# Two planner constants: chunk 0's tail admitted 34 steps before the end of attention, at 1,200 planned ns a block

## The chip, the core and the metric

The kernel runs as one program on one core of a Trainium2 chip. The engines are TensorE (PE, with its weight loads listed apart as PEld), VectorE (DVE), ScalarE (ACT), GpSimd (POOL) and SyncE (SP, which here only issues DMAs). The metric is the device time of one execution in microseconds; all times below are microseconds unless marked ns.

## The reference

For `x` of 2048 rows by 512 columns, six rows of modulation come from a condition vector: `sa, ca, ga, sb, cb, gb = silu(c) @ w_mod`. Then there are two halves.

```python
h = layernorm(x) * (1 + ca) + sa
x = x + ga * attention(h)          # 32 heads of width 16, then @ wo
h = layernorm(x) * (1 + cb) + sb
x = x + gb * mixer(h)

# mixer(h):
g  = gelu(layernorm(h) @ w1)
h1 = h + shift(g) @ w2             # the four column quarters moved by +1, -1, +2, -2 rows
return h1 + gelu(layernorm(h1) @ w3) @ w4
```

## The kernel before, in words

**Chunks, units, steps, blocks.** The 2048 rows are four chunks of 512 queries. Attention handles one chunk and one pair of heads at a time: a unit, 64 in all, chunk 3's last. A unit is 16 steps, one for each 128 keys, and a step has two halves, one for each head. The main loop takes three halves at a time; I call that a block. A block issues on PE the score matmuls of its halves (`sc`, L1012), the matmuls that find the row maxima 24 steps ahead (`mb`, L996), and then matmuls of probabilities and values (`pv`, L1086 for the high parts, L1083 for the low parts) of steps that lie two blocks back. ACT takes the exponential of each `sc` (L1008), DVE the maximum of each `mb` (L992), and each step needs one more pass that cuts out the low part of the probabilities, `p_low`: on POOL (L1061) or on ACT (L156), wherever the planner's clock is ahead. L1083 reads what that pass writes. In the last 24 steps there is no `mb` any more.

**The tail.** What comes after attention is done chunk by chunk by the generator `tail(ci)`. Chunk 0's begins inside attention. It transposes chunk 0's attention output (`xT<-ident,osb`, L1247; ACT L353 and DVE L349 split each result in two parts), multiplies by `wo` (48 matmuls `wo`, lines 359, 361 and 363 in turn, twelve for each of four row tiles that I number 0 to 3), and runs a chain for each row tile on DVE, POOL and ACT: add (L1406), statistics (L370, L371, L1353), POOL's power `trs` (L1356), centring (L1415), scaling (L1418), statistics again, POOL L1356, L1360 and L1361, and ACT's `xn` (L1367). Two row tiles together are then transposed (`xT<-ident,xn`) and multiplied by `w1` (matmuls named `w`, twelve for each bank of results). Each bank goes through the gelu chain: ACT square L1456, DVE L1457, ACT tanh L1458, DVE L1438, ACT copy L1459, POOL L1460. The three buffers for `xn` make row tile 3 wait in the plan until row tiles 0 and 1 have been transposed.

**Order.** All engines' programs are written out by a planner, `Sched`, which keeps a clock for each engine and puts operations in the order in which it thinks they will be ready. On the chip each engine runs its program in that order and waits on semaphores. Between blocks the planner may put in pieces of the generators, on credit: every block adds to `due`, and when `due` reaches a threshold, `fill(due)` lets the generators issue about so many ns of TensorE work.

```python
late = s0 >= NS - T0S
due += RATE3 if late else RATE if s0 < NS // NC else RATE2
if due >= (BURST3 if late else BURST if s0 < NS // NC else BURST2):
    sch.fill(due)
    due = 0.0
...
if blk and blk[0] <= 2 * (NS - T0S) <= blk[-1]:
    sch.add(tail(0))
```

`NS` is 1024 steps, `BURST3` is 1300, so that with 1,000 or 1,200 a block every second block has a fill. A generator that is not ready (a buffer taken, a flag not set, no PSUM bank) gives nothing, whatever the credit. Banks are shared: seven rotate among `sc`, `mb` and what the generators use.

**Names of blocks.** I count blocks back from the last one with scores, block 0 (it has two `sc`). Before the change the first fill with tail work stands at the end of block -20, and block -16 is the last with `mb`.

Of the kernel before, what the change touches and what calls it, by code (L numbers as in the profile page):

```python
# [82 lines left out]
X1T = 5  # L83
XBF = 4
XBT = 4
T0S = 30
T0L = 140
T0W = 3000.0
RATE3 = 1000.0
BURST3 = 1300.0  # L90
BF, BR = 2, 3
HOME = "rfrr"
# [238 lines left out]
def kernel(ctx, tc, A_x, A_wqkv, A_wo, B_w1, B_w2, B_w3, B_w4, c, w_mod, out):  # L331
# [942 lines left out]
    def tail_loads():  # L1274
        rings["0"] = Ring(FRONT, [], "r")
        for _ in range(BR):
            rings["0"].add([("wr", BR)])
            yield sch.wait(T0W)
        for t in range(TPC):
            x1t[t] = fa.tile([P, D], F32, name="x1", tag="x1", bufs=X1F)  # L1280
            act.dma_start(x1t[t], x_d[t * P:(t + 1) * P])
# [320 lines left out]
    for k, blk in enumerate(blocks + [[]] * (LAG + CPER)):  # L1602
# [52 lines left out]
        elif sch.gens:  # L1655
# [3 lines that stand above are left out]
# [14 lines left out]
        if blk and blk[0] <= 2 * (NS - T0L) <= blk[-1]:  # L1673
            sch.add(tail_loads())
        if blk and blk[0] <= 2 * (NS - T0S) <= blk[-1]:
            sch.add(tail(0))
# [54 lines left out]
```

## Time and profile before

| | us |
|---|---|
| median of three runs | 2020.98 |
| lowest and highest run | 2018.84 and 2023.25 |
| the profiled execution, its own time | 2021.44 |
| its span, first to last instruction | 2019.7 |
| PE busy | 1934.4 (96%) |
| DVE busy | 1656.3 (82%) |
| POOL busy | 1571.9 (78%) |
| ACT busy | 1510.2 (75%) |

The span has three parts: the projections up to about 100, attention to about 1533, and the tails of the four chunks. A row of the timeline gives the start, the duration, the engine, the line and operation, the tiles, the shapes and the count, and in brackets how long the engine stood idle before it and what released it. A row of a view by windows gives the stretch, its length, each engine's busy time with its number of instructions, the granted clock of TensorE as a share of full speed, the share of the DMA engines and GB/s.

### The profile page before, as it was taken

The numbers are of one execution on the slowest core, as the hardware profiler recorded it, in microseconds if no ns is written. First come the engines' busy times: TensorE is split into PE (matmuls) and PEld (weight loads), VectorE is DVE, ScalarE is ACT, GpSimd is POOL, SyncE is SP. The second block draws the span as 40 slices with busy tenths as digits, with TensorE's granted clock in tenths as the row PEclk, the third lists the DMA queues.
The fourth block names the chain that finished last, engine by engine and source line by source line (L and its number), as shares of the span: only waits on it lengthen the run. The fifth ranks groups of instructions, "written<-read, shape, count | busy, mean of one in ns | idle before, by whom it ended". The sixth has DMA issues, their size and how long they took to land.

```text
span 2019.7 us, 41655 instructions
## 1 busy us (share of the span) xinstructions
PE 1934.4 (96%) x14456; PEld 1162.1 (58%) x14456; DVE 1656.3 (82%) x2979; ACT 1510.2 (75%) x3085; POOL 1571.9 (78%) x1488
## 2 busy tenths in 40 slices
PE   7999999999999999999999999999998999999999
PEld 5755545454444444444444444444455878898998
DVE  6398888879999999999999999999975886556443
ACT  6438987768999999999999999999985544344443
POOL 6349988879999999999999999999996554435222
PEclk9989999999999999999999999999999999999999
DMA  8777675445343434444443435354414676553541
GB/s 295 233 204 192 151 187 155 135 130 124 86 92 87 91 88 83 96 82 97 81 98 75 104 72 107 72 136 126 99 46 158 230 261 265 226 200 116 201 153 68
DMA packets 185508, 278.01 MB, mean 138 GB/s; under 512 B 117104, under 2 KB 127856, under 8 KB 169008
## 3 DMA queue, kind: packets, MB, share of 16 engines
q1 hardware_dynamic: 181792, 267.20, 49.1%
q10 hardware_dynamic: 2304, 4.20, 0.6%
q0 software_dynamic: 1200, 3.93, 0.5%
q8 instruction: 115, 1.88, 0.4%
q14 instruction: 97, 0.79, 0.1%
HBM read 211.81 MB, written 62.91 MB: 136 GB/s over the span
## 4 chain that ended last, share of the span: by engine, by line
PE 61%; DVE 16%; ACT 9%; issue 6%; POOL 4%; DMA 3%; SPq 0%; ACTq 0%; POOLq 0%; DVEq 0%
PE mb L996 13%; DVE mx L992 12%; PE pv L1086 9%; PE sc L1012 8%; ACT pt L1008 7%; PE w L363 5%; PE w L359 5%; PE w L361 5%; PE pv L1083 4%; PE ot L1113 3%; POOL pt L1061 2%; PE xT L1247 1%; POOL trs L1356 1%; PE v L359 1%; DMA wr<-Ws 1%
## 5 line engine op out<-in xcount | busy, mean ns | idle before, releaser
L1061 POOL TENSOR_SCALAR pt<-pt 128x1024 f16<-128x1024 uint16 x953 | 1248.3, 1367 | 79.9 <-ACT pt L1008 76.7
L992 DVE TENSOR_REDUCE mx<-mb 128x1 f32<-128x512 f32 x2048 | 1250.0, 681 | 72.7 <-PE mb L996 63.5
L1008 ACT ACTIVATE pt<-sc 128x512 int32<-128x512 f32 x2048 | 1060.9, 614 | 123.5 <-PE mb L996 97.1
L996 PE MATMUL mb<-kst,qtl 62*128 62x512 f32 x2048 | 781.1, 461 | 20.5 <-ACT pt L1008 10.0
L1012 PE MATMUL sc<-qtl,kst 64*128 64x512 f32 x2048 | 739.3, 449 | 4.6 <-DVE mx L992 1.8
L996 PEld LDWEIGHTS mb<-kst,qtl 62*128 62x128 f32 x2048 | 358.9, 193 | 233.7 <-ACT pt L1008 160.4
L1012 PEld LDWEIGHTS sc<-qtl,kst 64*128 64x128 f32 x2048 | 336.6, 185 | 185.4 <-DVE mx L992 118.7
L1086 PE MATMUL pv<-pt,vst 128*32 128x512 f16 x4096 | 384.8, 397 | 20.6 <-ACT ac L1103 20.6
L1460 POOL TENSOR_TENSOR g<-sq,g 128x256 fp32r<-128x256 f32 (+1 forms) x124 | 96.8, 785 | 188.9 <-ACT g L1459 176.6
L1083 PE MATMUL pv<-pt,vst 128*32 128x512 f16 (+1 forms) x2048 | 220.8, 389 | 2.5 <-POOL pt L1061 2.4
L1086 PEld LDWEIGHTS <-vst 128*32 128x32 bf16 x4096 | 91.8, 93 | 227.2 <-issue 208.8
L361 PE MATMUL w<-A,wr 128*128 128x256 f32 (+1 forms) x520 | 153.4, 295 | 0.3 <-DVE A L349 0.3
L359 PE MATMUL w<-A,wr 128*128 128x256 f32 (+1 forms) x520 | 153.2, 295 | 0.3 <-ACT A L353 0.3
L363 PE MATMUL w<-A,wr 128*128 128x256 f32 (+1 forms) x520 | 153.1, 294 | 0.0
L1456 ACT ACTIVATE sq<-w 128x256 f32<-128x256 f32 (+1 forms) x130 | 52.1, 401 | 127.0 <-PE w L363 117.5
L363 PE MATMUL w<-wr,g 128*128 128x512 f32 x270 | 106.5, 394 | 3.1 <-POOL g L1460 3.1
L359 PE MATMUL w<-wr,g 128*128 128x512 f32 x270 | 106.9, 396 | 1.8 <-DMA wr<-Ws 1.8
L361 PE MATMUL w<-wr,g 128*128 128x512 f32 x270 | 106.1, 393 | 0.0
L1438 DVE SCALAR_TENSOR_TENSOR sq<-sq,w 128x256 f32<-128x256 f32 (+1 forms) x130 | 58.1, 449 | 56.5 <-ACT sq L1458 56.3
L359 PEld LDWEIGHTS w<-A,wr 128*128 128x128 f32 x520 | 98.7, 190 | 1.7 <-ACT A L353 0.5
L361 PEld LDWEIGHTS w<-A,wr 128*128 128x128 f32 x520 | 98.7, 190 | 1.6 <-DVE A L349 0.5
L363 PEld LDWEIGHTS w<-A,wr 128*128 128x128 f32 x520 | 98.6, 190 | 0.5 <-issue 0.5
(156 smaller groups left out, 2131.6 us busy)
## 6 DMA issues: line engine op xcount, KB each, us to landing
wr<-Ws SPq DMA_DIRECT2D x66, 1024.0 KB, 5.2
vst<-Vs SPq DMA_DIRECT2D x64, 768.0 KB, 5.7
kst<-Ks SPq DMA_DIRECT2D x126, 384.0 KB, 6.1
Ws<-wr SPq DMA_DIRECT2D x14, 1024.0 KB, 5.0
qtl<-Qs SPq DMA_DIRECT2D x128, 96.0 KB, 4.3
Vs<-vt SPq DMA_DIRECT2D x32, 384.0 KB, 4.2
Ks<-qk SPq DMA_DIRECT2D x16, 512.0 KB, 3.8
Qs<-qk SPq DMA_DIRECT2D x16, 512.0 KB, 3.0
```

The source lines that it names most:

```text
L359: te.matmul(o, lh, rh, start=first, stop=False)
L361: te.matmul(o, lh, rl, start=False, stop=False)
L363: te.matmul(o, ll, rh, start=False, stop=last)
L992: end = sch.crit("D", 605, e + PX, lambda: dve.reduce_max(mxs[u][:, j, g, c:c + 1], b, axis=AX.X))
L996: return ready, lambda: te.matmul(b, lhs, kst[u % 3][r, c * CH:(c + 1) * CH], start=True, stop=True), after
L1008: ea = sch.crit("A", 480, e + PX, lambda: act.activation(pt[s][:, j], b, AF.Exp))
L1012: return ready, lambda: te.matmul(b, kst[u % 3][r, kt * P:(kt + 1) * P], qst[u][r], start=True, stop=True), after
L1061: e_low[s] = XP["G"] + sch.crit("G", 1345, ready, lambda: pool.tensor_scalar(o, i, 0.5, 1.0, op0=OP.mult, op1=OP.mult))
L1083: te.matmul(acc[r:r + n, :], v[:, kt + i, c:c + n].bitcast(F16), pt[s + i].bitcast(F16)[:, j, 0::2], start=False, stop=kt == NKT - 2, skip ...
L1086: te.matmul(acc[r:r + 32, :], v[:, kt, r:r + 32], pt[s].bitcast(F16)[:, j, 1::2], start=kt == 0, stop=False, skip_group_check=True)
L1113: te.matmul(b[:, t * n:(t + 1) * n], ac[:, t * P:(t + 1) * P], smat.rearrange("p j d -> p (j d)"), start=True, stop=True)
L1460: ("G", cG(n), lambda: pool.tensor_tensor(lo, sq, hi, op=OP.subtract)), (None, 0, end), bank=b)
```

## The change

```diff
-T0S = 30
+T0S = 34
...
-RATE3 = 1000.0
+RATE3 = 1200.0
```

`T0S` sets both when `tail(0)` is admitted and when the credit rate becomes `RATE3`. The instructions are the same except for one `p_low`, which is on ACT (L156) now and was on POOL (L1061). Their order differs only from block -21 to a few microseconds after block 0; before and behind that, every engine's program is the same but for numbers in names of buffers.

PE, the end of block -17 and the start of block -16 (`osb` is chunk 0's attention output), first before and then now:

```order
L1083 MATMUL pv<-pt,vst 32x512
L1247 MATMUL xT<-ident,osb_105 128x128 x7
L1012 MATMUL sc<-qtl_1103,kst_1105 128x512
L996 MATMUL mb<-kst_147,qtl_145 128x512 x2
L1012 MATMUL sc<-qtl_1103,kst_1105 128x512 x2
```

```order
L359 MATMUL wo<-wr,A 128x512
L361 MATMUL wo<-wr,A 128x512
L363 MATMUL wo<-wr,A 128x512
L1012 MATMUL sc<-qtl_1103,kst_1105 128x512
L996 MATMUL mb<-kst_147,qtl_145 128x512 x2
L1012 MATMUL sc<-qtl_1103,kst_1105 128x512 x2
```

The rows of `wo` are the last three of nine, which with a unit's `ot` (L1113) before them now stand ahead of block -16; the `ot` stood one block earlier. The sixteen transposes of `osb` stood 5, 3, 1 and 7 behind blocks -20, -19, -18 and -17, and stand 8, 5 and 3 behind blocks -21, -20 and -19 now. The 48 `wo` stood 9, 9, 9, 9, 9 and 3 behind blocks -15, -13, -11, -9, -3 and -1, and stand 9, 11, 11, 5, 11 and 1 behind blocks -17, -15, -13, -11, -3 and -1 now. The eight transposes of `xn` of row tiles 0 and 1 stood behind block -5 and stand four each behind blocks -7 and -6 now. From the fifth `w` that stood behind the last `pv` on, PE's program is the same again: twelve `w` stood between the last `pv` and the following `ot`, and eight do now.

ACT in blocks -7 to 0 (`ot`, `sm` are a unit's closing sums), before and now:

```order
L1120 ACTIVATE sm<-ot 128x136
L1008 ACTIVATE pt<-sc 128x512 x6
L353 ACTIVATE A<-xT 128x2x256 x2
L1008 ACTIVATE pt<-sc 128x512 x6
L1367 ACTIVATE xn<-xb,trs 128x512
L1008 ACTIVATE pt<-sc 128x512 x8
```

```order
L1120 ACTIVATE sm<-ot 128x136
L353 ACTIVATE A<-xT 128x2x256
L1008 ACTIVATE pt<-sc 128x512 x3
L156 ACTIVATE pt<-pt 128x1024
L1367 ACTIVATE xn<-xb,trs 128x512
L353 ACTIVATE A<-xT 128x2x256
L1008 ACTIVATE pt<-sc 128x512 x15
```

The `p_low` of a step of block -7 stands on ACT now, among the exponentials of the next block, and POOL has one fewer.

DVE at the end of attention, from the add of row tile 3 (`x_21950`) on; `w_24626`, `w_24671` (`w_24672` before) and `w_24685` are the first, second and third bank of `w1` results. Before and now:

```order
L1406 TENSOR_TENSOR x_21950<-x_21950,wo 128x512
L370 BN_STATS tst<-x_21950 128x6
L371 BN_AGGR tmv<-tst 128x2
L1353 TENSOR_SCALAR tmv<-tmv 128x1
L1415 SCALAR_TENSOR_TENSOR xb<-x_21950,tmv,cbrow 128x512
L1457 SCALAR_TENSOR_TENSOR sq<-sq,w_24626 128x256
L1457 SCALAR_TENSOR_TENSOR sq<-sq,w_24672 128x256
L1418 SCALAR_TENSOR_TENSOR xb<-xb,trs,sbrow 128x512
L1438 SCALAR_TENSOR_TENSOR sq<-sq,w_24626 128x256
L1438 SCALAR_TENSOR_TENSOR sq<-sq,w_24672 128x256
L370 BN_STATS tst<-xb 128x6
```

```order
L1406 TENSOR_TENSOR x_21950<-x_21950,wo 128x512
L1457 SCALAR_TENSOR_TENSOR sq<-sq,w_24626 128x256
L1438 SCALAR_TENSOR_TENSOR sq<-sq,w_24626 128x256
L1457 SCALAR_TENSOR_TENSOR sq<-sq,w_24671 128x256
L370 BN_STATS tst<-x_21950 128x6
L371 BN_AGGR tmv<-tst 128x2
L1353 TENSOR_SCALAR tmv<-tmv 128x1
L1415 SCALAR_TENSOR_TENSOR xb<-x_21950,tmv,cbrow 128x512
L1438 SCALAR_TENSOR_TENSOR sq<-sq,w_24671 128x256
L1418 SCALAR_TENSOR_TENSOR xb<-xb,trs,sbrow 128x512
L1457 SCALAR_TENSOR_TENSOR sq<-sq,w_24685 128x256
```

Row tile 3's first statistics stood directly behind its add and stand behind three gelu operations of the first two banks now; its second statistics follow the third bank's L1438 now. ACT's `xn` of row tile 3 stands behind the fourth bank's L1459 now, and stood ahead of its L1458.

## The prediction

> **What bounds the kernel now.** I read the engines' busy time by windows first, then POOL's `p_low`, then the timeline of PE, DVE and ACT around the end of attention. First comes a stretch inside attention, second the last 40 us up to POOL's last `p_low`; the third row counts `p_low` alone in that stretch (POOL busy, clock, DMA), the fourth is the page's group of all of them.
>
> ```profile
> 1440.00:1460.00 20.00, 19.53 (x171) 9.19 (x170) 19.39 (x35) 18.25 (x38) 19.63 (x18) 1.00 0.38 81
> 1493.30:1533.30 40.00, 37.82 (x276) 19.75 (x276) 18.42 (x36) 26.82 (x54) 39.30 (x41) 1.00 0.25 79
> ```
>
> ```profile
> 1493.30:1533.30 40.00, 33.34 (x24) 1.00 0.25 79
> ```
>
> ```profile
> L1061 POOL TENSOR_SCALAR pt<-pt 128x1024 f16<-128x1024 uint16 x953 | 1248.3, 1367 | 79.9 <-ACT pt L1008 76.7
> ```
>
> While maxima are still taken, PE (19.5 of 20), DVE (19.4) and POOL (19.6) are all near full. In the last 40 us of attention DVE falls to 18.4 of 40, ACT to 26.8, PE stays at 37.8, and POOL is full: 39.3, of it 33.3 in 24 `p_low`, 1.39 each. So in this stretch POOL's queue sets the end of attention, and PE's fills run beside it. What the change can move is decided there and in the few microseconds behind.
>
> More planned credit does not mean more tail work ahead of the end: the program of PE is the same again four matmuls behind the last `pv`, so nothing substantial leaves the time after attention. The change reorders, and each reordering has a price.
>
> **Part 1: fills before block -16 make POOL wait.** The timeline of PE and POOL around block -16 before, and one pair of ACT rows for the lag from scores to exponentials:
>
> ```profile
> 1485.18 1.08 PE L1113 MATMUL ot<-smat,ac 128*128 128x34 f32 x8
> 1488.11 0.98 PE L1247 MATMUL xT<-ident,osb 128*128 128x128 f32 x7
> 1489.02 0.49 PE L1012 MATMUL sc<-qtl,kst 64*128 64x512 f32 x1
> 1491.87 0.50 PE L359 MATMUL wo<-wr,A 128*128 128x512 f32 x1
> 1494.14 0.73 PE L1012 MATMUL sc<-qtl,kst 64*128 64x512 f32 x3
> ```
>
> ```profile
> 1488.36 0.40 POOL L1124 TENSOR_TENSOR osb<-sm,rc 128x128 f32<-128x128 f32 x1 [1.75 <-DVE rc L1128]
> 1488.73 3.92 POOL L1061 TENSOR_SCALAR pt<-pt 128x1024 f16<-128x1024 uint16 x3
> 1493.12 0.20 POOL L1045 TENSOR_TENSOR nm<-mf,nm 128x8 fp32r<-128x8 f32 x1 [0.47 <-ACT nm L1044]
> 1493.30 6.60 POOL L1061 TENSOR_SCALAR pt<-pt 128x1024 f16<-128x1024 uint16 x5
> 1530.99 0.95 POOL L1356 TENSOR_TENSOR trs<-tmv,mhalf 128x1 f32<-128x1 f32 x1
> 1531.92 1.35 POOL L1061 TENSOR_SCALAR pt<-pt 128x1024 f16<-128x1024 uint16 x1
> ```
>
> ```profile
> 1494.73 3.05 ACT L1008 ACTIVATE pt<-sc 128x512 int32<-128x512 f32 x6 [1.69 <-PE sc L1012]
> ```
>
> Block -16 starts at 1489.02. Its `p_low` is the third of the three from 1488.73, so it began at 1488.73 + 2 x 1.31 = 1491.3. Now nine `wo` stand ahead of the block, 1494.14 - 1491.87 = 2.27 here. The same sixteen transposes and one `ot` stand ahead of it as before, but eight transposes at once hold two PSUM banks while ACT and DVE are full, so the next blocks' sixth matmul waits for a bank; following the banks I get 0.9 more (bounds 0, and 1.75, POOL's largest wait in the rows above). Block -16 then starts at 1489.0 + 2.3 + 0.9 = 1492.2; its second exponential ends 0.59 + 2 x 0.51 later, at 1493.8. POOL's `p_low` starts there: 2.5 late (bounds 1.4 and 3.4).
>
> Against that POOL loses one `p_low` and no longer has row tile 3's `trs` (0.95) ahead of the last one. Before, 24 `p_low`, the `nm` and the small operations ran from 1493.12 to 1531.92 + 1.35 = 1533.27. Now 24 run from 1493.8, the `nm` included, without that `trs`: 1493.8 + 40.15 - 0.95 = 1533.0, and I take 1533.1 since the add, centring and scaling on DVE collide with POOL as often as before. The moved `p_low` lies on ACT beside 13 us of idle time and costs nothing; without that cover it would be 1.4. POOL's end is thus unchanged within 0.2 (bounds -1.2 and +0.8). SP's row loads that hang on the `nm` go out 5 us later, and their readers, block -10's scores, start later too, some 2 us behind the landing: free.
>
> **Part 2: row tile 3's chain.** PE, DVE and ACT from the last fill (behind block -1) to the transposes of `xn`:
>
> ```profile
> 1527.46 0.50 PE L359 MATMUL wo<-wr,A 128*128 128x512 f32 x1
> 1528.03 0.40 PE L363 MATMUL wo<-wr,A 128*128 128x512 f32 x1
> 1529.65 0.50 PE L1012 MATMUL sc<-qtl,kst 64*128 64x512 f32 x2
> 1531.11 0.39 PE L363 MATMUL w<-A,wr 128*128 128x256 f32 x1
> 1533.09 0.64 PE L1083 MATMUL pv<-pt,vst 128*32 128x512 f16 x4
> 1536.01 0.36 PE L359 MATMUL w<-A,wr 128*128 128x256 f32 x1
> 1537.41 0.28 PE L363 MATMUL w<-A,wr 128*128 128x256 f32 x1
> 1539.93 1.09 PE L1247 MATMUL xT<-ident,xn 128*128 128x128 f32 x8 [2.25 <-DVE sq L1438]
> ```
>
> ```profile
> 1528.46 0.69 DVE L1406 TENSOR_TENSOR x<-x,wo 128x512 f32<-128x512 f32 x1 [7.49 <-PE wo L363]
> 1529.18 0.69 DVE L370 BATCH_NORM_STATS2 tst<-x 128x6 f32<-128x512 f32 x1
> 1530.20 1.32 DVE L1415 SCALAR_TENSOR_TENSOR xb<-x,tmv,cbrow 128x512 f32<-128x512 f32 x1
> 1533.37 0.42 DVE L1457 SCALAR_TENSOR_TENSOR sq<-sq,w 128x256 f32<-128x256 f32 x1 [1.00 <-ACT sq L1456]
> 1533.71 0.75 DVE L1418 SCALAR_TENSOR_TENSOR xb<-xb,trs,sbrow 128x512 f32<-128x512 f32 x1
> 1534.37 0.75 DVE L1438 SCALAR_TENSOR_TENSOR sq<-sq,w 128x256 f32<-128x256 f32 x2
> ```
>
> ```profile
> 1533.83 0.42 ACT L1458 ACTIVATE sq<-sq 128x256 f32<-128x256 f32 x1 [0.18 <-DVE sq L1457]
> 1538.30 0.81 ACT L1367 ACTIVATE xn<-xb,trs 128x512 f32<-128x512 f32 x1 [0.19 <-POOL trs L1361]
> ```
>
> The last fill follows the `pv` that waits for POOL's fifth-last `p_low`. With POOL's end at 1533.1, four `p_low` of 1.33 behind it and 0.4 to the fill, it starts at T = 1528.2, 0.7 later than 1527.46; but one `wo` is left of it, not three, so row tile 3's add can start at T + 0.5 = 1528.7 against 1528.46.
>
> From there, by the rows: the second bank's last `w` is 24 matmuls at 0.12 behind that `wo`, with block 0's scores and `pv` between (1531.11 - 1529.65 = 1.46): done at T + 4.9. ACT's square (0.4) and DVE's L1457 (0.4) follow, so the first statistics, which now stand behind it, start at T + 5.8, where before they started 0.7 behind the add. Statistics to centring 1.0 (1530.20 - 1529.18), centring 0.75 (as scaling; the 1.32 has POOL in its way), L1438 0.4, scaling 0.75: T + 8.7. The third bank is caught in between: L1459 on ACT (0.4) to T + 8.35, then its square, L1457, tanh and L1438 in turn between ACT and DVE, 4 x 0.43, to T + 10.1; only now the second statistics, 1.1, to T + 11.2. The fourth bank's L1457, tanh, L1438 and L1459 take 4 x 0.44 to T + 12.95 (POOL's `trs` runs beside it), `xn` 0.81: T + 13.75. The transposes start at T + 13.8 = 1542.0, against 1539.93: **2.1 later**. PE has its last `w` done at about T + 9.8, so it stands idle 4.0 there, against 2.25. Bounds: if DVE's waits overlap as before, the chain is no longer than it was, and only T counts (+0.3 for the add); if POOL's end is at its upper bound and block 0 waits for it, +3.4.
>
> **Part 3: what follows.** Behind the transposes every engine's order is as before, and the waits that PE has in the tails are on products of its own earlier work:
>
> ```profile
> PE xT L1247 <- ACT xn L1367: 14.1, 9, 2.9
> ```
>
> That is 14.1 in nine waits, the longest 2.9. So I carry the delay to the end in full. The sum: POOL 0, row tile 3 +2.1, one execution of 2021.44 becomes 2023.5. That execution lies 0.46 above the median of the runs, 2020.98, so the forecast is 2023.1, or 0.10% more. Less than 0.2%, about 4 us, a measurement of this kernel can hardly tell from no change.
>
> **The rivals.** *A longer idle gap halves the clock (slower).* The rows of the tail where PE last stood idle, and what followed:
>
> ```profile
> 1559.00:1563.00 4.00, 0.36 (x2) 0.14 (x1) 3.90 (x9) 2.89 (x5) 3.42 (x7) 1.00 0.00 0
> 1563.00:1569.50 6.50, 5.63 (x19) 4.86 (x20) 4.66 (x7) 3.41 (x6) 4.17 (x3) 0.50 0.99 354
> ```
>
> After 4 us with 0.36 of PE work the granted clock was 0.50 for 6.5 us, with PE busy 5.6: about 2.8 lost. Waits up to 2.9 elsewhere in the tail brought no such stretch. The new gap of 4.0 lies between 2.9 and this case, and if the chain is 0.8 longer than worked out it is clearly as long. Then the time is 2.1 + 2.8 = 4.9 above, 2025.9. [...] For it speaks the size of the gap, against it that the gap could turn out nearer 3.
>
> *POOL isn't made late (faster).* If block -16's exponentials come in time (before 1491.4, so with the `wo` hidden), POOL's end is 2.5 earlier, and T with it; with the chain lengthened as above that leaves 2020.6, and with a chain of the old length 2018.5. If besides the stretch at half clock that follows 1563 doesn't come in its new place, 2.8 less, 2015.7. Against it speaks that PE is already at 19.5 of 20 in that stretch.
>
> *It doesn't do anything that lasts.* The 2.1 is absorbed by a later wait, such as one for weights; 2021.0. Against it: those loads are released by PE's own progress.
>
> **How the numbers follow.** Forecast 0.42, its own range 2020.5 to 2025.5; half clock 0.32; POOL not late 0.16; absorbed 0.10. Slower by over 0.2% (above 2025.0): nearly all of the half-clock case (0.30) and the upper end of the forecast's (0.11), 0.41. Faster by over 0.2% (below 2016.9) needs the old chain and the missing half-clock stretch together, half of the faster rival's chance: 0.08. Within: 0.51. The range from 2017.5 to 2027.5 takes in the faster rival's 2018.5 with 1 for the bounds of POOL's lateness (3.4 instead of 2.5), and the half-clock case with 1.6 for its unknown chain.
>
> **What would show it.** Right: POOL idle some 2 us before the `p_low` near 1494, 952 on POOL and 72 on ACT; last `pv` within 1 of 1533; transposes of `xn` x8 near 1542, released by ACT's `xn` and not DVE's L1438, after about 4 idle; a constant shift from there on. Wrong: if the last `pv` moves by more than 1.5 (part 1), if the transposes come before 1540.5 (part 2), if the shift changes behind 1545 without a change of clock (part 3).

## The result, and the profile after

| kernel | median | lowest to highest | runs |
|---|---|---|---|
| before | 2020.98 | 2018.52 to 2024.23 | 5 |
| changed | 2028.28 | 2022.76 to 2033.27 | 5 |

The ratio of changed to before is 1.0041, with a 95% interval from 1.0026 to 1.0056: slower, by 7.3 in the medians. The forecast was 2023.1 with a range up to 2027.5, so the time went the way that was forecast, but by more than three times as much. The profiled execution of the changed kernel has its own time of 2028.28 and a span of 2026.5.

The mean granted clock of an execution goes with most of the spread in its time. The changed kernel's five had 0.992, 0.988, 0.987, 0.986 and 0.983, with 2022.76, 2028.00, 2028.28, 2030.83 and 2033.27. Of 120 executions of the kernel before that were made beside the experiments, 79 had 0.991 or 0.992 (median 2019.98) and 10 had 0.988 or less (median 2026.93); a line through all of them has 1.4 for each 0.001.

So the first view to read is the clock. The windows of the changed kernel below are 3.41 long, because its stretches at half clock last 3.41, 6.83, 10.24 or 17.07. The columns are the window, its length, busy time of PE, PEld, DVE, ACT and POOL, then the clock, DMA share and GB/s.

```profile
1504.54:1507.95 3.41, 1.82 (x15) 0.61 (x15) 1.90 (x5) 2.64 (x6) 3.24 (x5) 1.00 0.00 0
1507.95:1511.36 3.41, 3.11 (x20) 0.94 (x19) 2.62 (x3) 3.26 (x7) 3.41 (x4) 0.52 0.00 0
...
1521.60:1525.02 3.42, 3.42 (x17) 1.55 (x18) 0.00 (x0) 2.21 (x5) 3.42 (x4) 0.50 0.02 5
1525.02:1528.43 3.41, 3.41 (x21) 1.94 (x19) 0.00 (x0) 0.58 (x2) 0.94 (x1) 0.98 0.26 91
```

One window with 1.82 of PE work is followed by five at half clock, 17 us, in the middle of attention's last blocks. In the kernel before, the clock was 1.00 there:

```profile
1504.54:1528.43 23.89, 21.71 (x158) 10.59 (x159) 9.55 (x20) 18.33 (x37) 23.56 (x27) 1.00 0.13 45
```

These are rows from the timelines of PE, POOL and ACT in blocks -9 and -8, changed kernel:

```profile
1505.57 0.41 PE L1083 MATMUL pv<-pt,vst 128*32 128x512 f16 x3 [0.27 <-POOL pt L1061]
1505.90 0.73 PE L1012 MATMUL sc<-qtl,kst 64*128 64x512 f32 x3
1506.68 0.19 POOL L1361 TENSOR_SCALAR trs<-trs 128x1 f32<-128x1 f32 x1
1506.91 0.81 ACT L1367 ACTIVATE xn<-xb,trs 128x512 f32<-128x512 f32 x1 [0.77 <-POOL trs L1361]
1507.63 0.57 ACT L1103 ACTIVATE ac<-pv 128x512 f32<-128x512 f32 x1
1508.25 0.62 PE L1086 MATMUL pv<-pt,vst 128*32 128x512 f16 x4 [1.62 <-ACT ac L1103]
1508.80 1.22 PE L1012 MATMUL sc<-qtl,kst 64*128 64x512 f32 x3
```

And the same place before the change:

```profile
1506.99 0.41 PE L1083 MATMUL pv<-pt,vst 128*32 128x512 f16 x3 [0.45 <-POOL pt L1061]
1507.33 0.50 PE L359 MATMUL wo<-wr,A 128*128 128x512 f32 x1
1507.54 0.64 ACT L1103 ACTIVATE ac<-pv 128x512 f32<-128x512 f32 x1
1509.27 0.39 PE L363 MATMUL wo<-wr,A 128*128 128x512 f32 x1
1509.59 0.73 PE L1012 MATMUL sc<-qtl,kst 64*128 64x512 f32 x3
```

A unit ends behind block -9: the next `pv` has to wait until ACT has copied out the old one (`ac`), and on ACT that copy stands behind an `xn`, which waits for POOL. Before, nine `wo` lay over this wait. Now the fills have used them up by block -11, row tile 3 may not start, and PE stands idle for 1.62.

Two other places are as the prediction had them. Block -16 (PE, POOL):

```profile
1485.66 0.48 PE L359 MATMUL wo<-wr,A 128*128 128x512 f32 x1
1487.91 0.49 PE L1012 MATMUL sc<-qtl,kst 64*128 64x512 f32 x1
1489.74 3.94 POOL L1061 TENSOR_SCALAR pt<-pt 128x1024 f16<-128x1024 uint16 x3 [2.80 <-ACT pt L1008]
```

The end of attention (PE), and the two groups of `p_low`:

```profile
1529.94 0.50 PE L363 MATMUL wo<-wr,A 128*128 128x512 f32 x1
1542.61 0.48 PE L1247 MATMUL xT<-ident,xn 128*128 128x128 f32 x1 [3.12 <-DVE sq L1438]
1543.77 1.75 PE L1247 MATMUL xT<-ident,xn 128*128 128x128 f32 x7 [0.68 <-ACT xn L1367]
```

```profile
L1061 POOL TENSOR_SCALAR pt<-pt 128x1024 f16<-128x1024 uint16 x952 | 1245.5, 1364 | 87.6 <-ACT pt L1008 84.8
L156 ACT ACTIVATE pt<-pt 128x1024 f16<-128x1024 uint16 x72 | 99.2, 1377 | 0.0
```

POOL's idle time before `p_low` went from 79.9 to 87.6, 2.80 of it at block -16. Behind the gap near 1540 comes a second stretch at half clock (0.50 from 1542.2 to 1549.0).

To compare kernels I count from the start of block -21, up to which the programs are the same; it lay 4.2 earlier in the changed kernel's profile, which has no half-clock stretches at 303 and 730 in the unchanged part. The times are those of the timelines, in us behind that start. The fourth column of times is the start of the row with the last transposes of `xn` (x8 before and in spread_again, x7 in the others); the last is from there to the span's end. Each row is one execution: two profiles of the same kernel (changed and after_again) differ by 1.5 in the last column.

| kernel | block -16 | block -2 | end of last `pv` | last row of `xT` of `xn` | from there to the end |
|---|---|---|---|---|---|
| before | 12.3 | 47.1 | 57.0 | 63.2 | 479.8 |
| changed | 15.4 | 54.7 | 63.5 | 71.2 | 482.7 |
| after_again | 15.6 | 51.5 | 60.3 | 68.0 | 481.2 |
| after_fill8 | 15.4 | 49.5 | 58.2 | 66.0 | 481.2 |
| spread16 | 13.6 | 49.6 | 58.4 | 66.1 | 479.6 |
| spread_again | 15.4 | 50.7 | 61.4 | 61.4 | 482.8 |

Two fixed points behind attention serve further down, where the programs are the same again: a transpose of `xn` near 1583 and a matmul `w` near 1618, the 2,501st and the 2,301st of PE's matmuls from the end, added transposes not counted.

### The profile page after: what moved, and what is told of

Same layout as the page of the kernel before. It is cut to its first block, busy times and chain, and to the rows that moved or that the text cites. A ratio compares the mean times of both kernels' runs of the same rounds, so it can differ in the third digit from the quotient of the medians.

```text
span 2026.5 us, 41661 instructions
## 1 busy us (share of the span) xinstructions
PE 1940.5 (96%) x14456; PEld 1166.5 (58%) x14456; DVE 1657.2 (82%) x2979; ACT 1511.5 (75%) x3086; POOL 1570.8 (78%) x1487
## 4 chain that ended last, share of the span: by engine, by line
PE 61%; DVE 15%; ACT 10%; issue 6%; DMA 4%; POOL 3%; SPq 1%; ACTq 0%; POOLq 0%; DVEq 0%
PE mb L996 13%; DVE mx L992 12%; PE pv L1086 9%; PE sc L1012 9%; ACT pt L1008 7%; PE w L363 5%; PE w L359 5%; PE w L361 5%; PE pv L1083 4%; PE ot L1113 3%; PE xT L1247 1%; POOL pt L1061 1%; DMA raw<-in_B_w_dram 1%; DMA wr<-Ws 1%; POOL trs L1356 1%
## 5 line engine op out<-in xcount | busy, mean ns | idle before, releaser
L1061 POOL TENSOR_SCALAR pt<-pt 128x1024 f16<-128x1024 uint16 x952 | 1245.5, 1364 | 87.6 <-ACT pt L1008 84.8
L1438 DVE SCALAR_TENSOR_TENSOR sq<-sq,w 128x256 f32<-128x256 f32 (+1 forms) x130 | 58.2, 449 | 57.0 <-ACT sq L1458 56.8
```

Source lines behind the costliest of these rows:

```text
L1061: e_low[s] = XP["G"] + sch.crit("G", 1345, ready, lambda: pool.tensor_scalar(o, i, 0.5, 1.0, op0=OP.mult, op1=OP.mult))
```

## The experiments

Theory C: the loss comes from stretches at half clock, set off where PE is short of work. Theory S: it comes from the schedule at an unchanged clock (POOL late at block -16, the longer chain of row tile 3). The kernel before ran beside each group: its medians were 2019.98 (t0s34, rate1200, after_twice, before_twice), 2020.78 (after_warm, before_warm, rate_warm, after_spread), 2020.17 (after_again, after_fill8, after_ln, spread16_ln) and 2020.80 (spread16, spread_again). In each table of results the ratio is against those.

**The two numbers apart: t0s34 and rate1200.**

```diff
 T0S = 34
-RATE3 = 1200.0
+RATE3 = 1000.0
```

> T0S = 34 with RATE3 = 1,000: chunk 0's tail is let in as early as in the changed kernel, each fill has as much as before. Seven wo stand ahead of block -16 (nine in the changed kernel, none before), two behind block -9 (none; nine before), and the end of attention has before's order of row tile 3. Theory C (the half-clock stretch behind block -9, set off by too little PE work there, makes the loss): two wo fill only 0.5 of the 1.6 us that PE waited for the copy of pv, so the stretch still comes in about half of the executions; median 2023 to 2027, mean clocks 0.987 to 0.992. Theory S (fills ahead of block -16 make POOL late, and row tile 3's chain is longer, at an unchanged clock): block -16 is late by 2.5, row tile 3 as before; 2022.5 to 2023.5 with a mean clock of 0.992 in all runs.

```diff
-T0S = 34
+T0S = 30
 RATE3 = 1200.0
```

> RATE3 = 1,200 with T0S = 30: no wo stands ahead of block -16, eleven stand behind each of blocks -15, -13 and -11, so only three are left behind block -9, and the second transposes of xn stand ahead of the last pv. Theory C: PE still runs short behind block -9, so the half-clock stretch comes in some executions: 2021 to 2026, and mean clocks that differ from run to run by up to 0.008. Theory S: POOL isn't late, so 2019 to 2021 at a mean clock of 0.992.

| kernel | median | runs | ratio and interval | mean clock |
|---|---|---|---|---|
| t0s34 | 2023.26 | 11 | 1.0017, 1.0005 to 1.0029 | 0.990 |
| rate1200 | 2020.25 | 12 | 0.9994, 0.9982 to 1.0006 | 0.991 |

The earlier start alone costs 3.3; the larger credit alone costs nothing that can be measured. The median of t0s34 lies in the ranges of both theories, but its clocks, 0.986 to 0.993, are not S's 0.992 in all runs. Its windows show the mark of C: a poor window in block -5 and two at half clock behind it. The wait there is another one, 1.29 for POOL's `p_low`:

```profile
1517.10:1520.50 3.40, 1.94 (x19) 0.90 (x10) 1.89 (x4) 1.61 (x4) 3.40 (x4) 1.00 0.00 0
1520.50:1527.30 6.80, 6.80 (x29) 3.35 (x27) 0.69 (x1) 5.15 (x9) 6.28 (x8) 0.50 0.01 2
```

The median of rate1200 lies in S's range and below C's. Yet its profile has one window at half clock in attention, from 1513.0, behind a wait of 1.09 for `p_low`. So not every stretch there shows in the median.

**PE kept busy by scores that are issued twice: after_twice and before_twice.**

```diff
-te.matmul(b, kst[u % 3][r, kt * P:(kt + 1) * P], qst[u][r], start=True, stop=True)
+for _ in range(2 if 2016 <= 2 * s + j < 2040 else 1):
+    te.matmul(b, kst[u % 3][r, kt * P:(kt + 1) * P], qst[u][r], start=True, stop=True)
```

> The changed kernel, in which each score matmul of blocks -10 to -3 is issued twice into the same bank (24 matmuls more, some 0.23 us each, 5.5 us of PE work in all; the results are the same). Theory C: PE stays busy enough in these blocks, the granted clock is 1.00 from 1490 to 1540, and the median falls by 4 or more in spite of the added work, to 2021 to 2024. Theory S: the clock played no part; the added work is hidden at best, 2028 to 2033.

> The kernel before with the same 24 score matmuls issued twice, a control. Theory C: there is no half-clock stretch there to be removed; the added 5.5 us lie mostly beside POOL's queue: 2020 to 2024. Theory S: the same. If this run falls by as much as the changed kernel with the same edit, the edit works in another way than by the clock.

| kernel | median | runs | ratio and interval | mean clock |
|---|---|---|---|---|
| after_twice | 2028.39 | 10 | 1.0039, 1.0026 to 1.0053 | 0.989 |
| before_twice | 2024.03 | 12 | 1.0013, 0.9999 to 1.0027 | 0.991 |

The clock of after_twice stayed at 1.00 through attention, as C said, and its last `pv` ended 58.6 behind block -21 instead of 63.5; the median did not fall, which S had said and C had not. Its profile has stretches at half clock behind 1540, 1563, 1608 and 1714. The control rose by 4 in the medians too (its ratio's interval takes in 1), though its last `pv` ended at 57.1, as without the edit. Its profile is longer where the program is the same: between the two fixed points it takes 39.3, and 35.3 before the edit, with a stretch at 1605 that the kernel before does not have. Why it comes is not shown.

**Poor places covered: after_warm, before_warm, rate_warm.** Besides the double scores (after_warm only), constants are transposed into a bank that the real transposes then overwrite: near 1540 twenty in after_warm, twelve in before_warm and none in rate_warm, near 1560 eight and eighteen in all three. The diff is that of after_warm.

```diff
+for _ in range(warm[i] if kk is ks[0] and not j else 0):
+    te.transpose(b[:, :P] if nt == 2 else b[:, 3 * P:], ident, ident)
 te.transpose(b3[:, j, i * P:(i + 1) * P], src(k, i), ident)
...
+warm = (0, 0, 0) if ci else (0, 8, 18) if key == "xn4" else (20 * i, 0)
```

> The changed kernel with PE kept at work in three places and nothing else changed: the scores of blocks -10 to -3 are issued twice (as in after_twice), twenty more transposes of a constant stand ahead of the transposes of xn of row tiles 2 and 3 (into a bank that they then overwrite), and eight and eighteen stand between the first transposes of the next xn (near 1560). In after_twice the clock held through attention, but the time stayed, with half-clock stretches at 1540 and later. Theory C (half-clock stretches make most of the loss, wherever PE has a wait of 2 to 5 us): with all three covered the mean clock rises to 0.991 or more and the median falls to 2022 to 2025; what is left over before_warm, about 3, is the schedule's own loss (block -16 late by 3.1, longer chain of row tile 3). Theory S (the clock doesn't matter, after_twice's time is the schedule's): 2028 to 2032.

> The kernel before with twelve more transposes of a constant ahead of the transposes of xn of row tiles 2 and 3, and eight and eighteen between the first transposes of the next xn. Theory C: the stretch at half clock from 1563 to 1570 goes, which cost about 2.8; mean clock 0.994, median 2016.5 to 2018.5. Theory S: 2020 to 2021, as before.

> RATE3 = 1,200 with T0S = 30, with the eight and eighteen more transposes of a constant near 1560 alone. Its own run had 2020.25 with a half-clock stretch from 1560.5 to 1568. Theory C: 2016.5 to 2018.5, mean clock 0.993 to 0.995. Theory S: 2020 to 2021.

| kernel | median | runs | ratio and interval | mean clock |
|---|---|---|---|---|
| after_warm | 2022.15 | 12 | 1.0009, 0.9999 to 1.0019 | 0.992 |
| before_warm | 2021.58 | 12 | 1.0001, 0.9991 to 1.0011 | 0.992 |
| rate_warm | 2021.97 | 12 | 1.0005, 0.9995 to 1.0015 | 0.992 |

The changed kernel with more work to do is 5 to 6 faster, and its clock in the last blocks is full:

```profile
1508.00:1525.00 17.00, 16.12 (x127) 8.98 (x131) 4.31 (x7) 14.40 (x28) 16.08 (x17) 1.00 0.12 38
```

But after_twice had a full clock there too, and its last `pv` ends at the same 58.6. So what after_warm gains over after_twice lies behind attention: its profile is 3.4 shorter from the end of the last transposes to the first fixed point (39.2 against 42.7), and 4.3 shorter from there to the second (34.6 against 38.9), where after_twice has stretches at 1564 and 1608. The pair fits C, for stretches behind attention; it does not price those inside it.

For the other two C was wrong about the time: the stretch that follows 1563 went in their profiles, and the medians lie above the ranges of both theories. The profiles say more. From the end of the last transposes to the first fixed point they take 39.3 (before_warm) against 41.9 (before), and 45.9 (rate_warm) against 47.8 (rate1200): 2.6 and 1.9 less without the stretch, not far from the 2.8 that I had reckoned. But the added transposes near 1540 cost before_warm 1.3 ahead of that, and rate_warm's profile is 4 longer between the fixed points, with stretches at 1599 and 1616. So these medians do not price the stretch at 1563. A stretch at 1583 costs nothing that shows: between the fixed points after_warm and before_warm, which have it, take 34.6 and 35.4, and the kernel before, which has not, 35.3.

The cover near 1540 was a miss, as PE's timeline in after_warm shows:

```profile
1538.34 4.00 PE L1252 MATMUL xT<-ident 128*128 128x128 f32 x20 [3.12 <-DVE sq L1445]
1542.13 1.15 PE L1253 MATMUL xT<-ident,xn 128*128 128x128 f32 x8
```

The added transposes wait as long as the real ones would, for a bank that DVE has to release, and then delay them.

**The wo spread out: after_spread, and once more as spread_again.** A matmul of `wo` may only be issued while the count is below a cap for its block.

```diff
...
+yield lambda: 12 * i + n < {17: 9, 16: 9, 15: 17, 14: 17, 13: 24, 12: 24, 11: 30, 10: 30}.get(len(blocks) - 1 - cur[0], 48)
...
```

> The changed kernel with its wo matmuls capped: 9, 9, 7, 6 and 5 stand behind blocks -17, -15, -13, -11 and -9 (9, 11, 11, 5 and 0 in the changed kernel); by the planner the fourth row tile then stands behind block -5, and the transposes of xn of row tiles 2 and 3 directly behind the last pv. Theory C: PE no longer runs short behind block -9, so the granted clock is 1.00 until the end of attention in most executions; block -16 is still late by 3. Median 2020 to 2024. Theory S: block -16's lateness and the order of the chains make the loss; 2025 to 2028.

> The kernel of after_spread once more (wo 9, 9, 7, 6 and 5), beside the same runs of the kernel before: whether its 2019.26 against 2020.78 is a gain. If it is: ratio 0.999 or less, interval below 1. If it was luck: 1.000 with an interval across it. Its first run says 0.9993, and nothing in it removes the lateness of block -16, so 0.9995 is expected, 2019 to 2021.

| kernel | median | runs | ratio and interval | mean clock |
|---|---|---|---|---|
| after_spread | 2019.26 | 12 | 0.9993, 0.9983 to 1.0003 | 0.992 |
| spread_again | 2020.75 | 11 | 1.0000, 0.9989 to 1.0011 | 0.992 |

Both new numbers with another distribution of the same matmuls: the loss is gone, and there is no gain; the 2019.26 of the first run did not come again. Block -16 is as late as in the changed kernel (15.4), so that lateness alone makes no loss here. But the planner also moved the transposes of `xn` to the last `pv` (they come 9.8 earlier than in the changed kernel), so this run does not price the lateness by itself.

**One wait alone: after_again and after_fill8.** The first is the changed kernel once more. The second issues the scores of block -8 three times, six matmuls where PE waited 1.62.

```diff
-te.matmul(b, kst[u % 3][r, kt * P:(kt + 1) * P], qst[u][r], start=True, stop=True)
+for _ in range(3 if 2022 <= 2 * s + j < 2025 else 1):
+    te.matmul(b, kst[u % 3][r, kt * P:(kt + 1) * P], qst[u][r], start=True, stop=True)
```

> The changed kernel once more, unaltered, for a second profile and more executions on the chip that the other three share. Theory C: half-clock stretches at the last blocks of attention and behind the gap near 1540 again, their number differing from one execution to the next: median 2026 to 2029, mean clocks from 0.984 to 0.992, and the time falls by about 1.2 for each 0.001 of mean clock. A rival, chance: the stretch from 1508 to 1525 was one odd execution; then the profile has a clock of 1.00 there and the median is about 2023, with a mean clock of 0.991.

> The changed kernel with the three score matmuls of block -8 alone issued three times each: six matmuls more, 1.4 us, at the place where PE waited 1.62 for the copy of pv. Theory C, in its narrow form (that one wait sets off the whole stretch): the clock holds through attention, the last pv comes 4 to 5 earlier, and the median falls by 2 to 5, to 2023 to 2026. In its wide form (PE has too little work in all of blocks -9 to -4, and another window falls short when this one doesn't): a shorter or later stretch, and a fall of 0 to 2. Theory S: no change, 2027 to 2029.

| kernel | median | runs | ratio and interval | mean clock |
|---|---|---|---|---|
| after_again | 2027.24 | 10 | 1.0034, 1.0021 to 1.0046 | 0.987 |
| after_fill8 | 2024.10 | 11 | 1.0020, 1.0009 to 1.0030 | 0.990 |

The second profile of the changed kernel has the same wait (1.62) and the same mark, with two windows at half clock instead of five:

```profile
1508.60:1512.00 3.40, 1.78 (x17) 0.83 (x16) 1.27 (x2) 2.61 (x6) 3.23 (x6) 1.00 0.00 0
1512.00:1518.90 6.90, 6.90 (x37) 3.58 (x37) 2.94 (x6) 4.27 (x10) 6.54 (x9) 0.52 0.00 0
```

In after_fill8 (PE's timeline, then two windows; the lines of the code lie three or four further down) the wait is down to 0.71 and attention keeps its clock, while the stretch near 1540 stays:

```profile
1506.68 1.65 PE L1015 MATMUL sc<-qtl,kst 64*128 64x512 f32 x9
1509.04 0.41 PE L1090 MATMUL pv<-pt,vst 128*32 128x512 f16 x4 [0.71 <-ACT ac L1107]
```

```profile
1510.00:1525.00 15.00, 14.52 (x110) 7.25 (x113) 3.76 (x7) 12.78 (x25) 14.54 (x15) 1.00 0.13 51
1540.00:1547.00 7.00, 6.57 (x30) 6.07 (x29) 2.13 (x4) 2.20 (x6) 0.00 (x0) 0.51 0.29 119
```

Six more matmuls take 3.1 off the median (4.0 off the mean), as the narrow form of C had said: with this one wait covered, the stretch is gone from the profile. That the wait always sets off a stretch is not so, as the next run's profile shows.

**Row tile 3's chain: after_ln, spread16_ln and spread16.** The first puts the chain first on its engines; the second does so with `wo` capped to 1, 9, 9, 9 and 8; the third has the cap alone, so that of the change only the order at the end of attention is left.

```diff
-if ch[3] in self.owner and ch[0] <= max(until, self.T[e]):
+if (ch[3] in self.owner or ch[2] < 0) and ch[0] <= max(until, self.T[e]):
...
-*normed("xn", t, r2), bank=b)
+*normed("xn", t, r2), bank=b, prio=-1 if not ci and i == 3 else 1)
```

> The changed kernel with row tile 3's chain put first on DVE, ACT and POOL whenever it is ready: its statistics stand directly behind its add again, its xn ahead of the second bank's gelu, and by the planner the last twelve w of the first two banks' row tiles stand behind the transposes of xn, so that PE has no gap near 1540. All else, the fills included, is as in the changed kernel. Theory C: the stretch at 1508 to 1525 stays in most executions, the one near 1542 goes (3 us), and the chain's 1.5 with it: 2022 to 2025. Theory S: the chain's 1.5 alone: 2026 to 2028.

> T0S = 34 and RATE3 = 1,200 with row tile 3's chain first as in after_ln, and wo capped so that one stands ahead of block -16, and 9, 9, 9 and 8 behind blocks -15, -13, -11 and -9, as before the change but for one. If the three losses that the runs so far show are all there is (block -16 late, PE short of work behind block -9, the gap near 1540), all three are gone, and the gap that the kernel before has near 1539 as well: 2015.5 to 2018.5, faster than both, with a mean clock of 0.992 to 0.995. If row tile 3's chain or the gap costs nothing in the end: 2019 to 2021, as before.

> T0S = 34 and RATE3 = 1,200 with wo capped so that one stands ahead of block -16 and 9, 9, 9 and 8 behind blocks -15, -13, -11 and -9; without row tile 3's chain first. Only the end of attention is as in the changed kernel: row tile 3's statistics behind three gelu operations, the gap near 1540. So this is the price of the changed order there alone. Theory: POOL not late, clock 1.00 through attention, transposes of xn 1.5 to 2 later than before the change and a half-clock stretch behind them; together 2 to 3 above the kernel before, 2022 to 2024. Rival (the later chain is taken up behind it): within 1 of the kernel before, 2019.5 to 2021.5.

| kernel | median | runs | ratio and interval | mean clock |
|---|---|---|---|---|
| after_ln | 2028.10 | 7 | 1.0032, 1.0017 to 1.0047 | 0.988 |
| spread16_ln | 2026.32 | 11 | 1.0029, 1.0015 to 1.0043 | 0.989 |
| spread16 | 2023.04 | 12 | 1.0017, 1.0005 to 1.0029 | 0.990 |

after_ln came out at the upper end of theory S's range, with C's gain missing; spread16_ln lies above both of its ranges. The profile of after_ln is its fastest execution (2025.23). It has the wait for `ac` behind block -9 too (1.64), and yet the clock is 1.00 through attention and the last `pv` ends at 58.2. Its timeline of PE shows where the wait near 1540 went:

```profile
1538.91 1.92 PE L1113 MATMUL ot<-smat,ac 128*128 128x34 f32 x8 [3.00 <-ACT ac L1103]
1540.63 1.74 PE L1247 MATMUL xT<-ident,xn 128*128 128x128 f32 x7
```

With `xn` first on ACT, the copy `ac` stands behind it and behind POOL's `trs`; `ot` on PE waits 3.00 for that copy, in place of the 3.12 for DVE. The gap moved by a few instructions and kept its size, and half clock followed it. spread16 has the gap in its old form (PE; the last row of `wo` and the transposes):

```profile
1526.54 0.50 PE L363 MATMUL wo<-wr,A 128*128 128x512 f32 x1
1539.22 0.46 PE L1247 MATMUL xT<-ident,xn 128*128 128x128 f32 x1 [3.12 <-DVE sq L1441]
1540.37 1.76 PE L1247 MATMUL xT<-ident,xn 128*128 128x128 f32 x7 [0.69 <-ACT xn L1367]
```

Its last transposes are 2.9 later than before the change, and its median is 2.2 higher: the theory's value, not the rival's. Not all of it is the order at the end, though: block -16 is 1.2 late in it (13.55 against 12.31), where the theory had it in time, and the last `pv` is 1.3 late.

## Why the prediction was wrong

**What bounds, and the step that failed.** "POOL's queue sets the end of attention, and PE's fills run beside it" is the step that failed. The prediction costed the new positions of `wo` where they were put (ahead of block -16) and not where they were taken from (behind block -9). They had covered a wait for `ac`, and PE was busy 21.71 of 23.89 there, at a clock of 1.00. Behind 1.62 us of bare waiting came 17 and 7 us at half clock in the two profiles of the changed kernel, and PE took POOL's place as the bound: it was busy 16.88 of 17.07 and 6.90 of 6.90, and POOL 14.35 and 6.54. The last `pv`, forecast not to move, ended 6.5 and 3.3 late. after_again against after_fill8 prices the wait at 3.1 in the medians; by the ratios, 1.0034 against 1.0020, 0.14%.

**Part 1.** Block -16 was put 3.2 late and was 3.1 late (15.4 against 12.3). POOL's `p_low` there was put 2.5 late and was 2.6 late, behind a wait of 2.80. The moved `p_low` is there, 952 and 72. The forecast of no change at the last `pv` was too low even at a full clock: in after_fill8 it ends at 58.2, against 57.0 before. spread16, with one `wo` ahead of block -16 instead of nine, has 58.4, so the nine don't explain it. The 0.9 that the prediction took for waits on banks at block -16 was measured by no run on its own; only the total of 3.1 was. The collisions of DVE with POOL were of this size in the profile before: L1418 took 1.78 at 1507.45, beside `p_low`, and 0.75 at 1533.71, with none beside it; but L1415 took 0.74 at 1504.98, beside `p_low` too.

**Part 2.** The transposes were put at T + 13.8, T being the start of the last fill. It started at 1529.94, and seven of the eight transposes at 1543.77: T + 13.83. They were released by ACT's `xn`; the first waited for a bank from DVE's L1438 until 0.7 before, which the prediction had not seen. The steps on the way agree too: row tile 3's first statistics were put at T + 5.8 and began at 1535.76, T + 5.82. So this part was right by its mechanism. Behind the last `pv` the transposes come 7.7, against 6.2 before. With the 1.3 by which the last `pv` is late, spread16 has 2.9 here, where 2.1 was forecast, and 2.2 in its median.

**Part 3 and the half-clock rival.** The rival's half clock came, at the gap it named (3.12 and 0.68 instead of 4.0; the clock was 0.50 for 6.8 behind it, and stayed at 1.00 behind the 2.25 before the change) and at a wait it did not name (1.62). Its chance of 0.32 was the author's estimate; in the profiles of the changed kernel, after_fill8 and spread16 half clock followed the gap each time. Its price of 2.8 looks too high at this gap: from the last transposes to the end, after_fill8 has 481.2 and before 479.8, 1.4 more, and spread16, with the same stretch, has nothing more. That is rough, since two profiles of the same kernel differ there by 1.5. In spread16 the shift of 2.9 was still 2.7 at the end. Half clock also came behind windows that were far from idle: those of 3.4 us with 1.82 (changed), 1.78 (after_again) and 1.94 (t0s34) of PE work were each followed by a clock of 0.50, for 17, 7 and 7 us.

**The sum.** 3.1 for the stretch in attention (after_fill8) and 2.2 for the changed order at the end (spread16) make 5.3 of the 7.1 to 7.3 between the medians; by the ratios, 0.14% and 0.17% of 0.34% to 0.41%. Up to 1.3 of spread16's 2.2 can come from its late last `pv`, and why that is late stays open. The rest is within the intervals. What the nine `wo` ahead of block -16 cost by themselves, and why the added scores of before_twice bring a stretch at 1605, stays open too. No version beat the kernel before beyond its interval; after_spread came nearest.

## What to carry to other kernels

When a change moves fill work, price the place that loses it first: list the waits that it covered there, and look at PE's busy share of each few microseconds once they are bare. An engine that is not the bound can become it: here PE's clock was 0.50 for 17 and 7 us behind a bare wait of 1.62, and covering that wait took 3.1 off the median. Moving one chain ahead on a queue moves whatever stands behind it as well: look at what it overtakes before calling the wait gone.

## What the runs showed of the hardware

The granted clock fell to 0.50 behind windows of 3.4 us in which PE was busy 1.78 (after_again), 1.82 (changed) or 1.94 us (t0s34), not only behind emptier ones (0.69, from 1538.80 to 1542.20 in the changed kernel). In the changed kernel's last blocks of attention it stayed there for 17.07 us although PE was busy 16.88 of them. The busy time of such a window alone does not tell what follows, since the kernel before kept its clock in the window behind this one with 1.86:

```profile
1580.07:1583.48 3.41, 1.86 (x14) 1.56 (x13) 1.84 (x5) 2.58 (x7) 2.15 (x4) 1.00 0.00 0
1583.48:1586.89 3.41, 3.41 (x22) 3.41 (x21) 3.22 (x7) 3.41 (x8) 2.37 (x2) 1.00 0.00 0
```

In the changed kernel's profile the stretches at half clock began at 33.51, 98.36, 135.91, 1508.06, 1542.20, 1566.09 and 1610.46: 19, 11, 402, 10, 7 and 13 times 3.413 apart. In after_ln the wait of 1.64 for `ac`, from 1510.75 to 1512.39, was not followed by half clock. The windows over it:

```profile
1507.96:1511.37 3.41, 2.50 (x18) 0.92 (x19) 2.58 (x7) 2.62 (x6) 3.24 (x6) 1.00 0.00 0
1511.37:1514.79 3.42, 2.25 (x20) 0.69 (x19) 1.94 (x2) 3.42 (x8) 3.42 (x4) 1.00 0.00 0
```

In the two profiles of the changed kernel the wait of 1.62 lies within the one window with 1.82 or 1.78 of work, but for 0.3 in the first. Why half clock followed there and not in after_ln was not shown: these are three executions, and no run moved the wait and left all else alone.

The same program differs from one execution to the next in how long it is at half clock: behind the same wait of 1.62 the changed kernel's two profiles had 17 and 7 us of it, with mean clocks of 0.987 and 0.989 and times of 2028.28 and 2025.97. A few microseconds between executions of one kernel go with the mean clock: 1.4 for each 0.001 over the 120 executions of the kernel before.
